# Mish layer on one core: the order of the first loads, with some of them behind TensorE's fillers

## The chip, the cores and the metric

The kernel runs on one core of a Trainium2 chip. A core has five engines, each with its own queue of instructions: TensorE (PE in the profile; PEld is its weight load), VectorE (DVE), ScalarE (ACT), GpSimd (POOL) and SyncE (SP). They meet only through semaphores. SP and ACT also issue DMAs; all of these run on the core's 16 DMA engines. The metric is the device time of one execution in microseconds, the median of several runs.

## The reference

```python
B, S, D, F = 1, 2048, 512, 1792          # all bfloat16
def reference(x, w1, b1, w2):
    h = jnp.einsum("bsd,df->bsf", x, w1) + b1
    sp = jnp.log1p(jnp.exp(-jnp.abs(h))) + jnp.where(h > 0, h, jnp.zeros_like(h))
    act = h * jnp.tanh(sp)
    return jnp.einsum("bsf,fd->bsd", act, w2)
```

A dense layer, the Mish activation, and a second dense layer. The first product contracts over D = 512, the second over F = 1792.

## The kernel before

**Tiles.** TensorE contracts over 128 partitions, so D is cut into KT = 4 slices (k 0 to k 3) and F into FT = 14 (f 0 to f 13). The 2048 rows of x are worked in four blocks of 512 (BLOCKS). For each block the first product makes, for every f, a tile of 128 values of F by 512 rows in one of the eight PSUM banks, with x transposed (xT) as the moving operand (mm1_step, L178). ScalarE adds b1 and applies Mish in one instruction and writes a_sb (mish, L161). The second product (mm2_step, L200) takes a_sb as weights, 128 rows at a time, and sums over the 14 f; VectorE copies the result out (put, L206), and a DMA stores it (L209).

**The order of work** is written out by hand: each engine has a Stream, which puts waits on semaphores into that engine's queue and gives each marked instruction a number. An engine works off its queue in order, so a wait holds all that stands behind it on the same engine.

**Loads.** All go through load (L85), which gives every DMA its own semaphore. SP's queue issues, in this order: x rows 0 to 255 as they are (x_nat), w1's k 1 for f 0 to 7, a DMA that transposes x rows 256 to 511 on the way into xT, w1's k 3 for f 0 to 7, b1, the rest of w1 (f 8 to 13, all k), w2, and three DMAs that transpose the other blocks of x. ACT's queue issues w1's k 0 and k 2 for f 0 to 7, once VectorE has zeroed b1_nat (t_bz, L102), and then loads the activation table (L125).

**The start on TensorE.** Eight matmuls on a constant (WARM: five of 512 columns, two of 256, one of 128; dummy, L131) fill the time until x is there. transpose_x (L147) then transposes x rows 0 to 255 with eight matmuls against an identity, and VectorE and ScalarE copy them from PSUM into xT (L152). The first block's first product starts on these rows, in an order that follows the loads (first): with k 0 four f on rows 0 to 127, the same four f on rows 128 to 255, then f 4 to 7 on both; with k 1 and then k 2 eight f on 256 rows each; then k 0, k 1 and k 2 on rows 256 to 511, eight f each; then k 3 on all 512 rows, whereupon Mish can run (spread_b1, L230 and L232, has spread b1 over the partitions by then). f 8 to 13 follow in the usual order (mm1), then the block's second product, and then the other three blocks.

Of the kernel before, what the change touches and what calls it, by code (L numbers as in the profile page):

```python
# [5 lines left out]
P = 128  # L6
SQ = 32
WARM = (512,) * 5 + (256,) * 2 + (128,)
# [24 lines left out]
def bass_standalone__dense_activation_mish__prompt_kernel(  # L33
# [8 lines left out]
    ACT = mybir.ActivationFunctionType  # L42
    ALU = mybir.AluOpType
    BF, F32 = dt.bfloat16, dt.float32
# [9 lines left out]
    OPEN = 8  # L54
    N0 = BLOCKS[0] // P

    with ExitStack() as es:
# [14 lines left out]
        ps = es.enter_context(nc.psum_tensor("ps", [P, 8, 512], F32))  # L72

        def sem(name):
            return es.enter_context(nc.semaphore(name))

        sp = Stream(nc.sync, None)
        pe = Stream(nc.tensor, sem("c_pe"))
        dve = Stream(nc.vector, sem("c_dve"))
        act = Stream(nc.scalar, sem("c_act"))  # L80
        pool = Stream(nc.gpsimd, sem("c_pool"))

        def load(q, dst, src, name, transpose=False):
            s = sem(name)
            (q.eng.dma_start_transpose if transpose else q.eng.dma_start)(dst, src).then_inc(s, 16)  # L85
            return (s, 16)

        def load_w1(q, ks, a, b):
            return load(q, w1_sb[:, ks, a * P:b * P], w1v[:, ks, a * P:b * P], "s_w1_%d_%d" % (ks.start, a))
# [6 lines left out]
        def load_part(q, k0, k1, a, b):  # L96
            t = load_w1(q, slice(k0, k1), a, b)
            for f in range(a, b):
                for k in range(k0, k1):
                    t_w1[k, f] = t  # L100

        t_bz = dve.mark(nc.vector.memset(b1_nat[:, :], 0.0))  # L102
        act.wait(t_bz)
        for k in (0, 2):
            load_part(act, k, k + 1, 0, OPEN)
        t_xn = load(sp, x_nat[:, :, :], x2[0:2 * P, :].rearrange("(p j) d -> p j d", p=P), "s_xn")
        load_part(sp, 1, 2, 0, OPEN)
        t_x23 = load(sp, xT[:, :, 2 * P:4 * P], x2[2 * P:4 * P, :], "s_x23", True)
        load_part(sp, 3, 4, 0, OPEN)
        sp.wait(t_bz)  # L110
# [11 lines left out]
        t_diff = pool.mark(pool.eng.iota(diff[:, :], pattern=[[1, P]], base=0, channel_multiplier=-1))  # L122
        dve.wait(t_diff)
        t_id = dve.mark(nc.vector.tensor_scalar(ident[:, :], diff[:, :], 0, None, ALU.is_equal))  # L124
        act.eng.preload_act_table(ACT.Mish)  # L125

        c_w = nc.const_aps.tensor(1.0, [P, P], BF)
        c_m = nc.const_aps.tensor(1.0, [P, 512], BF)

        def dummy(n):  # L130
            nc.tensor.matmul(ps[:, 7, 0:n], c_w, c_m[:, 0:n], start=True, stop=True)  # L131


        free = [[] for _ in range(8)]
        t_cp = {(j, k): t_x23 for j in (2, 3) for k in range(KT)}
# [2 lines left out]
        def transpose_x():  # L138

            pe.wait(t_xn, t_id)  # L140
            for bank, (eng, js, ks) in enumerate(((dve, (0,), (0,)), (act, (1,), (0,)), (dve, (0, 1), (1,)),
                                                  (act, (0, 1), (2, 3)))):
                n, m = len(ks), len(js)
                for i, k in enumerate(ks):
                    for h, j in enumerate(js):
                        lo = (i * m + h) * P
                        mm = nc.tensor.matmul(ps[:, bank, lo:lo + P], x_nat[:, j, k * P:(k + 1) * P], ident[:, :],  # L147
                                              start=True, stop=True)
                eng.wait(pe.mark(mm))
                dst = xT[:, ks[0]:ks[0] + n, js[0] * P:(js[-1] + 1) * P]  # L150
                src = ps[:, bank, 0:n * m * P].rearrange("p (k t) -> p k t", k=n)
                t = eng.mark(nc.vector.tensor_copy(dst, src) if eng is dve else act.eng.activation(dst, src, ACT.Copy))  # L152
                for k in ks:
                    for j in js:
                        t_cp[j, k] = t
                free[bank] = [t]
# [74 lines left out]
            dve.wait(t)  # L231
            return dve.mark(nc.vector.tensor_copy(b1_sb[:, :], b1_T[:, 0:FT]))  # L232

        for n in WARM:
            dummy(n)
        transpose_x()
        t_b1c = spread_b1()
        first(range(4), (0,), (0,))
# [48 lines left out]
```

## Time and profile before

| | |
|---|---|
| median of three runs | 104.51 us (104.5 to 105.24) |
| the profiled execution | 104.79 us |
| its span, first to last instruction | 103.4 us |
| TensorE busy | 100.3 us |
| ScalarE busy | 39.2 us |
| VectorE busy | 13.3 us |
| bytes by DMA | 7.94 MB |

The profile is of one execution. The span runs from the first to the last instruction; the rest of the time lies around it. Times in the views are microseconds from the span's start unless marked ns. A matmul's end in the profile is modelled, so the time from start to start says more of TensorE's pace than the length of one. An issue on SPq or ACTq lasts as long as the queue is taken up with it; the data arrive later, and the DMA view gives the time from issue to landing.

### The profile page before, as it was taken

The page shows a single profiled execution, that of the slowest core. Times are in us where ns is not written, and L with a number is a line of the kernel's source. Part 1 is how long each engine was busy: PE and PEld are TensorE (multiplying, and loading weights), DVE is VectorE, ACT ScalarE, POOL GpSimd, SP SyncE. Part 2 cuts the span into 40 slices and gives each one's busy share as a digit, 9 for nine tenths or more (in the row PEclk, how much of TensorE's full clock was granted, in tenths as well). Part 3 has the DMA queues.
Part 4 walks back from the last instruction along what each step waited for, and adds up shares of the span by engine and source line. Part 5 has one row for each costly group of instructions (what it writes and reads, how often), then busy time and mean ns, then how long its engine had stood idle before and what let it go on. Part 6 is the DMA issues. An engine that isn't in the chain of part 4 may idle for free.

```text
span 103.4 us, 1142 instructions
## 1 busy us (share of the span) xinstructions
PE 100.3 (97%) x497; PEld 49.1 (47%) x506; DVE 13.3 (13%) x26; ACT 39.2 (38%) x59; POOL 0.4 (0%) x5
## 2 busy tenths in 40 slices
PE   7999999999999999999999999999999999999992
PEld 2788444444444444444444444444444444444462
DVE  1203000211220000022220000022201000020223
ACT  2500999100037777100007777400005777700000
POOL 1000000000000000000000000000000000000000
PEclk9999999999999999999999999999999999999999
DMA  2999999991110000011011000001111000001111
GB/s 59 371 311 363 349 222 206 190 218 51 51 50 1 0 0 6 0 51 49 2 51 51 0 0 3 6 0 51 51 51 51 0 0 0 0 0 55 53 51 51
DMA packets 12833, 7.94 MB, mean 77 GB/s; under 512 B 7836, under 2 KB 12188, under 8 KB 12828
## 3 DMA queue, kind: packets, MB, share of 16 engines
q1 hardware_dynamic: 12396, 7.31, 27.4%
q10 hardware_dynamic: 432, 0.56, 1.6%
q8 instruction: 4, 0.07, 0.3%
q14 instruction: 1, 0.01, 0.0%
HBM read 3.94 MB, written 2.10 MB: 58 GB/s over the span
## 4 chain that ended last, share of the span: by engine, by line
PE 97%; issue 1%; DVE 0%
PE ps L178 47%; PE ps L200 47%; PE ps L131 3%; PE ps L147 1%; DVE o_sb L206 0%
## 5 line engine op out<-in xcount | busy, mean ns | idle before, releaser
L161 ACT ACTIVATE a_sb<-ps,b_sb 128x512 bf16<-128x512 f32 x56 | 37.1, 697 | 48.0 <-PE ps L178 42.8
L178 PE MATMUL ps<-xT,w_sb 128*128 128x512 bf16 (+2 forms) x247 | 49.0, 358 | 0.3
L200 PE MATMUL ps<-w_sb,a_sb 128*128 128x512 bf16 (+2 forms) x234 | 48.8, 367 | 0.2
L178 PEld LDWEIGHTS ps<-xT,w_sb 128*128 128x128 bf16 x252 | 24.5, 99 | 24.0
L200 PEld LDWEIGHTS ps<-w_sb,a_sb 128*128 128x128 bf16 x238 | 22.8, 98 | 26.0
L206 DVE CAST o_sb<-ps 128x512 bf16<-128x512 f32 (+2 forms) x17 | 11.2, 660 | 81.9 <-PE ps L200 81.9
L131 PE MATMUL ps<-const-bfloat16-1.0 128*128 128x512 bf16 (+2 forms) x8 | 2.8, 535 | 0.8 <-PEq L272 0.8
L131 PEld LDWEIGHTS ps<-const-bfloat16-1.0 128*128 128x128 bf16 x8 | 1.0, 140 | 2.2 <-issue 2.1
L125 ACT ACT_TABLE_LOAD x1 | 1.3, 1283 | 1.8 <-DVE ident L124 1.8
L152 ACT ACTIVATE xT<-ps 128x128 bf16<-128x128 f32 (+1 forms) x2 | 0.9, 437 | 1.1 <-PE ps L147 1.1
L230 DVE STREAM_TRANSPOSE b_T<-b_nat 32x32 bf16<-32x32 bf16 x4 | 0.8, 202 | 3.3 <-DMA b_nat<-in_b_dram 3.2
L147 PE MATMUL ps<-ident,x_nat 128*128 128x128 bf16 x8 | 1.0, 311 | 0.0
L152 DVE CAST xT<-ps 128x128 bf16<-128x128 f32 (+1 forms) x2 | 0.7, 358 | 2.5 <-PE ps L147 2.4
L147 PEld LDWEIGHTS ps<-ident,x_nat 128*128 128x128 bf16 x8 | 0.8, 142 | 0.2 <-DMA x_nat<-in_x_dram 0.2
L124 DVE TENSOR_SCALAR ident<-diff 128x128 bf16<-128x128 int32 x1 | 0.2, 226 | 0.2 <-POOL diff L122 0.2
L122 POOL IOTA diff<- 128x128 int32 x1 | 0.2, 234 | 0.4 <-POOLq L272 0.4
L102 DVE MEMSET b_nat<- 32x64 uint32 x1 | 0.1, 112 | 0.8 <-PEq L272 0.8
L232 DVE CAST b_sb<-b_T 128x14 f32<-128x14 bf16 x1 | 0.2, 175 | 0.0
L272 POOL MEMSET const-bfloat16-1.0<- 128x1 bf16 x1 | 0.1, 101 | 0.0
L272 POOL MEMSET const-uint8-127<- 128x1 uint8 x1 | 0.1, 101 | 0.0
L272 POOL MEMSET const-float32-0.0<- 128x1 f32 x1 | 0.1, 98 | 0.2 <-issue 0.2
L272 POOL MEMSET const-float32-1.0<- 128x1 f32 x1 | 0.1, 98 | 0.0
## 6 DMA issues: line engine op xcount, KB each, us to landing
out_dram<-o_sb SPq DMA_DIRECT2D x15, 128.0 KB, 1.7
w_sb<-in_w_dram SPq DMA_DIRECT2D x1, 1792.0 KB, 11.3
w_sb<-in_w_dram SPq DMA_DIRECT2D x1, 768.0 KB, 6.6
w_sb<-in_w_dram ACTq DMA_DIRECT2D x2, 256.0 KB, 3.8
w_sb<-in_w_dram SPq DMA_DIRECT2D x2, 256.0 KB, 4.0
x_nat<-in_x_dram SPq DMA_DIRECT2D x1, 256.0 KB, 2.6
out_dram<-o_sb SPq DMA_DIRECT2D x1, 96.0 KB, 1.6
xT<-in_x_dram SPq DMA_TRANSPOSE x4, 5.3
```

The costliest lines, as they stand in the source:

```text
L122: t_diff = pool.mark(pool.eng.iota(diff[:, :], pattern=[[1, P]], base=0, channel_multiplier=-1))
L124: t_id = dve.mark(nc.vector.tensor_scalar(ident[:, :], diff[:, :], 0, None, ALU.is_equal))
L125: act.eng.preload_act_table(ACT.Mish)
L131: nc.tensor.matmul(ps[:, 7, 0:n], c_w, c_m[:, 0:n], start=True, stop=True)
L147: mm = nc.tensor.matmul(ps[:, bank, lo:lo + P], x_nat[:, j, k * P:(k + 1) * P], ident[:, :], start=True, stop=True)
L152: t = eng.mark(nc.vector.tensor_copy(dst, src) if eng is dve else act.eng.activation(dst, src, ACT.Copy))
L161: t = act.mark(act.eng.activation(a_sb[:, f, starts[s]:starts[s + 1]], ps[:, bank, 0:n], ACT.Mish, bias=b1_sb[:, f:f + 1]))
L178: return nc.tensor.matmul(ps[:, bank, lo:hi], w1_sb[:, k, f * P:(f + 1) * P], xT[:, k, starts[s] + lo:starts[s] + hi], start=first, stop=( ...
L200: return nc.tensor.matmul(ps[:, bank, 0:hi - lo], a_sb[:, f, i * P:(i + 1) * P], w2_sb[:, f, lo:hi], start=(f == 0), stop=(f == FT - 1))
L206: t = dve.mark(nc.vector.tensor_copy(o_sb[:, i, lo:hi], ps[:, bank, 0:hi - lo]))
L230: t = dve.mark(nc.vector.transpose(b1_T[j * SQ:(j + 1) * SQ, :], b1_nat[:, j * SQ:(j + 1) * SQ]))
L272: nc = _bacc.Bacc("TRN2", target_bir_lowering=False, num_devices=1)
```

## The change

The table load becomes the first instruction on ACT. The eight fillers get a mark each, so that other engines can wait for them (t_fill). ACT still waits for the memset and issues k 0, but waits for the third filler before k 2. SP issues x_nat at once, waits for the second filler before k 1, and for the fifth before the DMA transpose; k 3, b1, the rest of w1, w2 and the other transposes stand behind that one as before. The fillers are put ahead in the program's text; on TensorE's queue they are first before and after. Nothing of the computation changes.

```diff
         t_bz = dve.mark(nc.vector.memset(b1_nat[:, :], 0.0))
+        c_w = nc.const_aps.tensor(1.0, [P, P], BF)
+        c_m = nc.const_aps.tensor(1.0, [P, 512], BF)
+
+        def dummy(n):
+            return nc.tensor.matmul(ps[:, 7, 0:n], c_w, c_m[:, 0:n], start=True, stop=True)
+
+        t_fill = [pe.mark(dummy(n)) for n in WARM]
+
+        act.eng.preload_act_table(ACT.Mish)
         act.wait(t_bz)
-        for k in (0, 2):
-            load_part(act, k, k + 1, 0, OPEN)
+        load_part(act, 0, 1, 0, OPEN)
+        act.wait(t_fill[2])
+        load_part(act, 2, 3, 0, OPEN)
         t_xn = load(sp, x_nat[:, :, :], x2[0:2 * P, :].rearrange("(p j) d -> p j d", p=P), "s_xn")
+        sp.wait(t_fill[1])
         load_part(sp, 1, 2, 0, OPEN)
+        sp.wait(t_fill[4])
         t_x23 = load(sp, xT[:, :, 2 * P:4 * P], x2[2 * P:4 * P, :], "s_x23", True)
         load_part(sp, 3, 4, 0, OPEN)
...
-        act.eng.preload_act_table(ACT.Mish)
-
-        c_w = nc.const_aps.tensor(1.0, [P, P], BF)
-        c_m = nc.const_aps.tensor(1.0, [P, 512], BF)
-
-        def dummy(n):
-            nc.tensor.matmul(ps[:, 7, 0:n], c_w, c_m[:, 0:n], start=True, stop=True)
...
-        for n in WARM:
-            dummy(n)
         transpose_x()
```

## The prediction, made before the result was known

> **What bounds the kernel now.** I read the page first, then the chain of waits in order of time, then the timeline of the first 16 us, then the DMA issues one by one.
>
> From the page: TensorE's share, its slices, and the DMA slices.
>
> ```profile
> PE 100.3 (97%) x497; PEld 49.1 (47%) x506; DVE 13.3 (13%) x26; ACT 39.2 (38%) x59; POOL 0.4 (0%) x5
> PE   7999999999999999999999999999999999999992
> DMA  2999999991110000011011000001111000001111
> ```
>
> From the chain of waits (start us, us, what):
>
> ```profile
> 0.73 0.04 issue
> 0.77 2.83 PE ps L131 x8
> 3.60 0.85 PE ps L147 x8
> 4.45 5.57 PE ps L178 x52
> 10.02 0.05 issue
> 10.07 6.86 PE ps L178 x31
> 16.93 3.88 PE ps L200 x18
> ...
> 101.59 0.02 issue
> 101.61 0.29 DVE o_sb L206
> ```
>
> The reader is to see that the chain never leaves TensorE: fillers (L131), transposes of x (L147), first product (L178), second product (L200), with nothing between them but gaps of 0.05 us, from 0.77 to 101.59 us. The 16 DMA engines are full until about 23 us (nine slices of 2.6 us). So the change can gain only if it makes TensorE start real work sooner, and it loses as soon as one load comes later than TensorE asks for it.
>
> This profiled execution took 104.79 us, 1.39 us of it outside the span of 103.4. The median of the runs is 104.51, so I add the change in the span to 104.51.
>
> **When each load is issued, when it lands, when it is asked for.** The timeline of the first 16 us (start us, us, engine, line, operation):
>
> ```profile
> 0.74 0.40 SPq L85 DMA_DIRECT2D x_nat<-in_x_dram  x1
> 0.95 0.87 ACTq L85 DMA_DIRECT2D w_sb<-in_w_dram  x2
> 1.20 0.41 SPq L85 DMA_DIRECT2D w_sb<-in_w_dram  x1
> 1.66 1.31 SPq L85 DMA_TRANSPOSE xT<-in_x_dram  x1
> 1.85 1.28 ACT L125 ACT_TABLE_LOAD   x1 [1.85 <-DVE ident L124]
> 3.02 0.57 SPq L85 DMA_DIRECT2D w_sb<-in_w_dram  x1
> 3.41 0.77 PEld L147 LDWEIGHTS ps<-ident,x_nat 128*128 128x128 bf16 x8 [0.19 <-DMA x_nat<-in_x_dram]
> 4.14 1.00 SPq L85 DMA_DIRECT2D w_sb<-in_w_dram  x2
> 4.26 12.02 PE L178 MATMUL ps<-xT,w_sb 128*128 128x128 bf16 x80
> 7.65 0.90 DVE L230 STREAM_TRANSPOSE b_T<-b_nat 32x32 bf16<-32x32 bf16 x4 [3.16 <-DMA b_nat<-in_b_dram]
> 8.59 0.17 DVE L232 CAST b_sb<-b_T 128x14 f32<-128x14 bf16 x1
> 10.34 5.88 ACT L161 ACTIVATE a_sb<-ps,b_sb 128x512 bf16<-128x512 f32 x10 [5.25 <-remote]
> ```
>
> The DMA view, asked around each issue in turn: x, w1's k 0, k 1, k 2, the DMA transpose of x rows 256 to 511, k 3, the rest of w1, w2. The last number is us from issue to landing.
>
> ```profile
> x_nat<-in_x_dram SPq DMA_DIRECT2D x1, 256.0 KB, 2.6
> w_sb<-in_w_dram ACTq DMA_DIRECT2D x1, 256.0 KB, 3.3
> w_sb<-in_w_dram SPq DMA_DIRECT2D x1, 256.0 KB, 3.7
> w_sb<-in_w_dram ACTq DMA_DIRECT2D x1, 256.0 KB, 4.4
> xT<-in_x_dram SPq DMA_TRANSPOSE x1, 5.0
> w_sb<-in_w_dram SPq DMA_DIRECT2D x1, 256.0 KB, 4.4
> w_sb<-in_w_dram SPq DMA_DIRECT2D x1, 768.0 KB, 6.6
> w_sb<-in_w_dram SPq DMA_DIRECT2D x1, 1792.0 KB, 11.3
> ```
>
> So x lands at 0.74 + 2.6 = 3.3, k 0 at 0.95 + 3.3 = 4.25, k 1 at 1.20 + 3.7 = 4.9, k 2 (the second of ACT's pair, about 1.4) at 5.8, the transposed rows at 1.66 + 5.0 = 6.7, k 3 at 7.4, the rest of w1 at 4.14 + 6.6 = 10.7, w2 (about 4.6) at 15.9.
>
> When TensorE asks for them follows from the shapes of the first products, here the matmuls grouped by form (busy us, mean ns), with the first row from 4.2 to 10 us:
>
> ```profile
> L178 PE MATMUL ps<-xT,w_sb 128*128 128x256 bf16 x44 | 5.0, 273 | 0.0
> L178 PE MATMUL ps<-xT,w_sb 128*128 128x128 bf16 x8 | 1.0, 297 | 0.0
> ```
>
> The 44 matmuls of 256 columns take 5.0 us, 0.113 each, and end where the chain has its gap at 10.02; so they began at 5.06. Four of them belong to k 0, then come 8 of k 1, 8 of k 2 and 24 on the transposed rows. k 1 is asked for at 5.06 + 4 x 0.113 = 5.5, k 2 at 6.4, the transposed rows at 7.3, k 3 at 10.07. In the chain from 10.07 eight matmuls of k 3 come ahead of the rest of w1; 31 take 6.86, so 8 take 1.77, and the rest of w1 is asked for at 11.8, w2 at 16.9. Slack today: k 1 0.6, k 2 0.6, transposed rows 0.6, rest of w1 1.1, w2 1.0. x and k 0 have none: k 0 lands as the first product starts.
>
> **The change part by part.**
>
> *The fillers and their marks.* The same eight matmuls stand first on TensorE before and after, and no queue is ahead of them; five semaphore marks more cost nothing that I can find a row for. Their price lies between 0 and the 0.05 of one of the chain's gaps; I take 0. Moving text that stands on other engines changes nothing on TensorE's queue.
>
> *x and k 0 alone at first.* x will land somewhat sooner than 3.3. What that can buy is the 0.19 us that the weight load waited for x at 3.41. But the matmuls were not idle then: the chain has the fillers and the transposes without a gap, and fillers stand ahead in the same queue. The gain lies between 0 and 0.19; I take 0. k 0 too may land sooner, and buys nothing: the transposes' eight matmuls end only as the first product starts.
>
> *The table load ahead of k 0 on ACT.* The load has 1.28 us and will start about 0.75, where the queues of SP and TensorE start. The trace of before has it behind the two DMA issues, never ahead, so it doesn't show whether a DMA issue waits for it. One end: it doesn't, and k 0 is issued at 0.95 as today, behind the same memset. Other end: it does, and k 0 is issued at 0.75 + 1.28 = 2.03. Then it lands 2.6 (x's row) to 3.3 (its own row) later, at 4.6 to 5.3, and the first product stalls 0.4 to 1.1. I take the first end, because the profile books the table load to the engine (ACT) and DMA issues to its queue (ACTq), two rows that need not wait for each other.
> [...]
>
> *k 1 behind the second filler, k 2 behind the third, the transpose behind the fifth.* Their ends, from the timeline asked at 1.25, 0 to 2, and 2.7 us:
>
> ```profile
> 0.77 1.01 PE L131 MATMUL ps<-const-bfloat16-1.0 128*128 128x512 bf16 x2 [0.77 <-PEq L272]
> 0.77 1.44 PE L131 MATMUL ps<-const-bfloat16-1.0 128*128 128x512 bf16 x3 [0.77 <-PEq L272]
> 2.43 0.64 PE L131 MATMUL ps<-const-bfloat16-1.0 128*128 128x512 bf16 x1
> ```
>
> Second at 1.78, third at 2.21, fifth at 3.07. So k 1 goes from 1.20 to 1.8, k 2 from 1.4 to 2.2, the transpose from 1.66 to 3.1. Behind the transpose on SP's queue stand k 3, b1, the rest of w1, w2 and three further transposes: all 1.41 later. Behind k 2's wait on ACT stand only the two copies of the transposed x at 3.85 and 4.49, over a us away.
>
> The late end: each load takes as long from issue to landing as today. k 1 lands at 5.5, asked for at 5.5: 0. k 2 at 6.6 against 6.4: 0.2. The transposed rows at 3.07 + 5.0 = 8.1 against 7.3: 0.8. k 3 at 8.8 against 10.07: 0. b1's spreading, which ended at 8.76, ends at 10.17, before the first activation at 10.34: 0. The rest of w1 at 12.1 against 11.8 and w2 at 17.3 against 16.9 are late by less than the 0.8 that the rows have by then put TensorE back. So the late end is 0.8 in all, not a sum.
>
> The early end counts bytes. Today those long times are mostly queueing, as the stretches of the start show (us, then busy times, last the DMA share and GB/s):
>
> ```profile
> 1.65:2.65 1.00, 1.00 (x4) 0.39 (x3) 0.00 (x0) 0.80 (x1) 0.00 (x0) 1.00 0.79 176
> 2.65:4.95 2.30, 2.30 (x19) 1.77 (x18) 0.72 (x2) 1.22 (x3) 0.00 (x0) 1.00 1.05 382
> 4.95:6.70 1.75, 1.75 (x20) 1.58 (x18) 0.00 (x0) 0.14 (x1) 0.00 (x0) 1.00 1.16 278
> ```
>
> 176 + 2.3 x 382 = 1055 KB by 4.95 is x, k 0, k 1 and k 2 (four times 262 KB). The transposed rows are today the fifth 262 KB, and stay so. If the engines never run dry, they end at 4.95 + 262/278 = 5.9, plus the time from the last byte to the semaphore, and land by about 6.7 as today. Do they run dry? A load's bytes start 0.9 us behind its issue (x: 0.74, first bytes at 1.65). x and k 0, 524 KB, last until 2.65 + 348/382 = 3.6; k 1 has bytes from 2.7, k 2 from 3.1, the transpose from 4.0, k 3 (issued 4.4) from 5.3, the rest of w1 (5.55) from 6.4. Each is there before the one ahead of it is through. So the early end is 0, and I take it: the rows of DMA share (1.05, 1.16) are nearer to a full queue than to a fixed latency. If that cover goes, the transposed rows are what is late first, at 7.3.
>
> **Sum.** 0 + 0 + 0 + 0: span 103.4, time 104.5. Between the ends of all parts: -0.19 to +1.1.
>
> **Rivals.**
> *Transposed rows late (slower).* Place: the 24 matmuls at 7.3. It decides once the rows land more than 0.6 later than now, that is if more than 0.6 of the 1.41 us of later issue comes through to the landing. For it: the issue alone takes 1.31 us, and nothing can be hidden twice. Against: the byte count. At its price, up to 0.8, the time is 105.3.
> *k 0 waits for the table load (slower).* Place: the first product at 4.26. It decides as soon as k 0 is issued more than a few hundredths later, as there is no slack. Price 0.4 to 1.1, middle 0.7: 105.2.
> [...]
> *A late clock.* From 4.26 on eight matmuls of 128 columns take from 4.26 to 5.06, 0.1 each, and then ones of 256 columns 0.113: TensorE doubles its pace at about 5.0, 4.2 us after its first filler. If a stall before 5.0 puts that step off by as much again, 4.2 us at half pace cost 2.1: with the 0.7 of the stall 107.3. [...]
> *A gain from earlier x.* The 0.19 comes through: 104.3. Against it the gapless chain at 3.4.
>
> **How the numbers follow.** No change 0.72 (its own range 104.2 to 104.9); transposed rows late 0.11; k 0 behind the table 0.10; ACT held twice as long 0.01; clock 0.02; gain 0.04. The range 104.2 to 105.4 takes in the likeliest, the gain, the late rows and over half of k 0's case. A measurement of this kernel can tell about 1%, 1.05 us. Faster by more than that (under 103.46): no case reaches it, 0.01. Slower (over 105.55): the clock, the long hold of ACT, the upper part of k 0's case, and a late load together with k 0, 0.10. Within: 0.89.
>
> **What the profile after would show.** Right: k 0 issued on ACTq at 0.95 beside the table load; no idle time on TensorE before 5.5 us; the transposed rows landing before 7.3, about 3.6 after their issue; the chain on TensorE alone. Wrong: ACTq's first issue at 2.0 and L178 waiting for w_sb at 4.3; or L178 waiting for xT at 7.3; or 256 columns taking over 0.2 us after 5.1; or, for a gain, L147 starting before 3.4.

## The result and the profile after

The changed kernel takes 105.82 us (median of 14 runs, 105.24 to 106.43); the kernel before, run beside it, 104.89 (14 runs, 104.35 to 105.64). The ratio is 1.0083, with a 95% interval of 1.0058 to 1.0108: slower by 0.9 us, less than 1% but clear of noise. The forecast was no change, 104.5 in 104.2 to 105.4, and the time lies outside that range. The profiled execution took 106.0 us with a span of 104.7.

The chain of waits of the changed kernel:

```profile
0.73 0.04 issue
0.77 1.03 PE ps L107 x2
1.80 0.02 issue
1.82 4.86 DMA w_sb<-in_w_dram
6.67 0.05 issue
6.72 4.54 PE ps L182 x40
11.26 0.05 issue
11.31 6.85 PE ps L182 x31
18.17 3.88 PE ps L204 x18
```

Where the chain was TensorE alone, it now goes from the second filler (L107) into a load of w1 that takes 4.86 us, and from that into the first product (L182). The timeline names the load and shows what became of each issue:

```profile
0.73 1.28 ACT L111 ACT_TABLE_LOAD   x1 [0.73 <-PEq L274]
0.95 1.63 ACTq L85 DMA_DIRECT2D w_sb<-in_w_dram  x2
1.82 0.33 SPq L85 DMA_DIRECT2D w_sb<-in_w_dram  x1
3.10 1.31 SPq L85 DMA_TRANSPOSE xT<-in_x_dram  x1
3.42 0.71 PEld L151 LDWEIGHTS ps<-ident,x_nat 128*128 128x128 bf16 x8 [0.20 <-DMA x_nat<-in_x_dram]
4.20 1.08 PE L182 MATMUL ps<-xT,w_sb 128*128 128x128 bf16 x12
6.72 9.50 PE L182 MATMUL ps<-xT,w_sb 128*128 128x256 bf16 x62 [1.44 <-DMA w_sb<-in_w_dram]
```

k 0 is issued at 0.95 beside the table load, as forecast. The twelve matmuls of k 0 run from 4.20 to 5.28. Then TensorE stands still for 1.44 us and begins k 1 at 6.72. The load is k 1, issued at 1.82. The DMA view, asked around each issue (x, k 0, k 1, k 2, the DMA transpose; last the us from issue to landing):

```profile
x_nat<-in_x_dram SPq DMA_DIRECT2D x1, 256.0 KB, 2.6
w_sb<-in_w_dram ACTq DMA_DIRECT2D x1, 256.0 KB, 3.1
w_sb<-in_w_dram SPq DMA_DIRECT2D x1, 256.0 KB, 4.9
w_sb<-in_w_dram ACTq DMA_DIRECT2D x1, 256.0 KB, 4.7
xT<-in_x_dram SPq DMA_TRANSPOSE x1, 4.7
```

k 1 needed 3.7 us when it was issued at 1.20, and needs 4.9 when it is issued later, with no more queued ahead of it. x, now with k 0 alone beside it, still needs 2.6. The stretches of the start, first of the changed kernel and then of the kernel before (last the DMA share and GB/s, both counted by the packets that start in the stretch):

```profile
1.65:2.65 1.00, 1.00 (x4) 0.39 (x3) 0.00 (x0) 0.36 (x1) 0.00 (x0) 1.00 0.44 170
2.65:3.65 1.00, 1.00 (x7) 0.53 (x6) 0.00 (x0) 0.00 (x0) 0.00 (x0) 1.00 1.00 373
3.65:4.65 1.00, 1.00 (x17) 0.97 (x16) 0.72 (x2) 0.58 (x2) 0.00 (x0) 1.00 0.87 145
4.65:5.65 1.00, 0.63 (x7) 0.28 (x4) 0.00 (x0) 0.29 (x1) 0.00 (x0) 1.00 1.14 366
5.65:6.65 1.00, 0.00 (x0) 0.00 (x0) 0.00 (x0) 0.00 (x0) 0.00 (x0) 1.00 1.11 162
```

```profile
2.65:3.65 1.00, 1.00 (x7) 0.54 (x6) 0.00 (x0) 0.48 (x1) 0.00 (x0) 1.00 1.04 379
3.65:4.65 1.00, 1.00 (x12) 0.93 (x11) 0.72 (x2) 0.44 (x2) 0.00 (x0) 1.00 1.06 401
4.65:5.65 1.00, 1.00 (x13) 0.94 (x11) 0.00 (x0) 0.44 (x1) 0.00 (x0) 1.00 1.16 267
5.65:6.65 1.00, 1.00 (x12) 0.90 (x10) 0.00 (x0) 0.00 (x0) 0.00 (x0) 1.00 1.18 314
```

Until 3.65, x and k 0, the two kernels move the same. Then, where k 1 should follow, the engines move 145 GB/s in place of 401, although k 1 had been issued 1.8 us earlier; 256 KB are missing by 4.65, the size of one load. A DMA share of 0.87 with 145 GB/s says that the engines are busy with packets that last long, not that they have none. The trace's packet records, read one by one, bear this out. In both kernels the first packets of k 1 start at 3.5 us. Of the 71 packets of 2 KB that start from 3.65 to 4.65 in the changed kernel, 52 take the usual 0.08 to 0.09 us, but 15 take 0.3 us or more, up to 1.07; in the kernel before 196 start there, and the longest takes 0.27. A second poor stretch follows at 5.65.

### The profile page after: what moved, and what is told of

The parts are those of the page before. It is cut to its first block, busy times and chain, and to the rows that moved or that the text cites. A ratio compares the mean times of both kernels' runs of the same rounds, so it can differ in the third digit from the quotient of the medians.

```text
span 104.7 us, 1142 instructions
## 1 busy us (share of the span) xinstructions
PE 100.1 (96%) x497; PEld 48.7 (47%) x506; DVE 13.3 (13%) x26; ACT 39.3 (37%) x59; POOL 0.4 (0%) x5
## 4 chain that ended last, share of the span: by engine, by line
PE 92%; DMA 5%; issue 1%; DVE 0%
PE ps L204 46%; PE ps L182 45%; DMA w_sb<-in_w_dram 5%; PE ps L107 1%; DVE o_sb L210 0%
## 5 line engine op out<-in xcount | busy, mean ns | idle before, releaser
L182 PE MATMUL ps<-xT,w_sb 128*128 128x512 bf16 (+2 forms) x247 | 48.9, 355 | 1.7 <-DMA w_sb<-in_w_dram 1.4
L182 PEld LDWEIGHTS ps<-xT,w_sb 128*128 128x128 bf16 x252 | 24.2, 98 | 25.6 <-DMA w_sb<-in_w_dram 1.6
L107 PE MATMUL ps<-const-bfloat16-1.0 128*128 128x512 bf16 (+2 forms) x8 | 2.8, 535 | 0.8 <-PEq L274 0.8
L107 PEld LDWEIGHTS ps<-const-bfloat16-1.0 128*128 128x128 bf16 x8 | 1.0, 140 | 2.2 <-issue 2.1
L151 PE MATMUL ps<-ident,x_nat 128*128 128x128 bf16 x8 | 0.9, 279 | 0.0
L151 PEld LDWEIGHTS ps<-ident,x_nat 128*128 128x128 bf16 x8 | 0.7, 133 | 0.2 <-DMA x_nat<-in_x_dram 0.2
```

The costliest lines, as they stand in the source:

```text
L107: return nc.tensor.matmul(ps[:, 7, 0:n], c_w, c_m[:, 0:n], start=True, stop=True)
L182: return nc.tensor.matmul(ps[:, bank, lo:hi], w1_sb[:, k, f * P:(f + 1) * P], xT[:, k, starts[s] + lo:starts[s] + hi], start=first, stop=( ...
```

## The experiments

Each is the changed kernel with the edit shown, unless it says otherwise. The table sums them up: when k 1, k 2 and the transpose of rows 256 to 511 are issued, GB/s from 3.65 to 4.65 us, when k 1 and k 2 land (issue plus the DMA view's time), and the ratio to the kernel before on the same chip. Landings and GB/s are of one profiled execution each. The ratios of e2, e4, g2 and h1 rest on four executions, that of f4 on two, the others on six to fourteen.

| kernel | k 1 | k 2 | rows | GB/s | k 1, k 2 land | ratio (95% interval) |
|---|---|---|---|---|---|---|
| before | 1.2 | 1.4 | 1.7 | 401 | 4.9, 5.8 | 1 |
| changed | 1.8 | 2.2 | 3.1 | 145 | 6.7, 6.9 | 1.0083 (1.0058 to 1.0108) |
| e1 table only | 1.2 | 1.4 | 1.7 | 401 | 4.9, 5.7 | 1.0006 (0.9967 to 1.0045) |
| e2 k 1, k 2 wait | 1.8 | 2.2 | 2.2 | 268 | 5.2, 6.9 | 1.0121 (1.0059 to 1.0182) |
| e3 rows wait | 1.2 | 1.4 | 3.1 | 404 | 4.8, 5.5 | 1.0021 (0.9984 to 1.0058) |
| e4 plain rows | 1.8 | 2.2 | 3.1 | 186 | 6.4, 6.6 | 1.0107 (1.0053 to 1.0161) |
| e5 k 1, rows wait | 1.8 | 1.4 | 3.1 | 352 | 6.0, 5.8 | 1.0029 (0.9998 to 1.006) |
| e6 k 2, rows wait | 1.2 | 2.2 | 3.1 | 348 | 4.7, 5.6 | 1.0049 (1.0016 to 1.0081) |
| e7 both on SP | 1.8 | 2.2 | 3.1 | 178 | 6.0, 6.8 | 1.0051 (1.0022 to 1.0081) |
| e8 waits a filler sooner | 1.4 | 1.8 | 3.1 | 395 | 4.8, 5.6 | 1.0032 (1.0005 to 1.0059) |
| f1 swapped | 1.8 | 2.2 | 3.1 | 74 | 6.7, 6.9 | 1.0082 (1.0061 to 1.0103) |
| f2 waits a filler later | 2.2 | 2.7 | 3.1 | 154 | 6.4, 6.7 | 1.0081 (1.0051 to 1.0112) |
| f3 k 3 first | 1.8 | 2.2 | 3.1 | 279 | 6.7, 7.0 | 1.0111 (1.0078 to 1.0143) |
| f4 e2, plain | 1.8 | 2.2 | 2.2 | 133 | 6.7, 6.9 | 1.0127 (1.0058 to 1.0195) |
| g1 k 2 behind the fifth | 1.8 | 3.1 | 3.1 | 234 | 4.8, 6.6 | 1.0074 (1.0028 to 1.012) |
| g2 one load | 1.8 | 1.8 | 3.1 | 217 | 6.7 | 1.0108 (1.0039 to 1.0176) |
| g3 behind the first | 1.4 | 1.4 | 3.1 | 375 | 5.5, 5.7 | 1.0006 (0.9966 to 1.0046) |
| h1 spaced | 1.8 | 2.7 | 3.6 | 217 | 6.7, 7.4 | 1.0127 (1.0063 to 1.019) |

**Which wait costs the time (e1 to e4).** Two theories stood against each other. A: while SP issues the transpose, the engines hardly move data, and the fifth filler's wait has put that stretch upon k 1. B: k 1 and k 2 themselves are issued too late.

e1 is the kernel before with the table load alone moved:

```diff
+        act.eng.preload_act_table(ACT.Mish)
         act.wait(t_bz)
...
-        act.eng.preload_act_table(ACT.Mish)
```

> The kernel before with the table load alone put first on ACT; no wait on a filler. All theories: ACTq issues k 0 at 0.95 us as before, every load lands as before (k 1 by 4.9, transposed rows by 6.7), TensorE without idle time, ratio to the kernel before 1.000 within its interval. If the table load has a part in the loss, k 1 or k 0 lands later and the ratio is 1.003 or more.

As expected: k 0 is issued at 0.95, k 1 lands at 4.9, and the table load's place costs nothing that these runs can tell (the interval reaches from 0.9967 to 1.0045).

e2 takes the transpose's wait away, e3 leaves it as the only one:

```diff
-        sp.wait(t_fill[4])            # e2
-        sp.wait(t_fill[1])            # e3
-        act.wait(t_fill[2])           # e3
```

> The changed kernel without the wait for the fifth filler: k 1 and k 2 still wait for the second and third filler, the transpose follows k 1 on SP at about 2.15 us. Theory A (while SP issues a transpose, the 16 engines hardly move data, wherever that falls): the poor stretch moves from 3.7-4.6 to about 2.4-3.4 us, onto x and k 0; k 1 lands by 5.5, the first product may start some tenths late; ratio 1.000 to 1.006. Theory B (k 1 and k 2, issued late, leave the engines dry): k 1 lands at about 6.5 as in the changed kernel and TensorE waits over 1 us for it; ratio 1.008 or more.

> The changed kernel with the wait for the fifth filler alone: k 1 and k 2 are issued at about 1.2 and 1.4 us as before, the transpose at 3.1. Theory A: GB/s fall below 200 between 3.6 and 4.6 us as in the changed kernel, k 1 lands at 5.6 or later (asked for at 5.5), transposed rows at 7.6; ratio 1.003 to 1.009. Theory B: no poor stretch, k 1 by 4.9, transposed rows by 6.8; ratio 1.000.

e3 moves as much as the kernel before, here its stretches and its chain, with TensorE alone in it:

```profile
3.65:4.65 1.00, 1.00 (x12) 1.00 (x10) 0.72 (x2) 0.44 (x2) 0.00 (x0) 1.00 1.05 404
```

```profile
0.77 2.82 PE ps L107 x8
3.60 0.85 PE ps L149 x8
4.45 5.40 PE ps L180 x52
9.85 0.05 issue
9.90 6.96 PE ps L180 x31
```

e2 is as slow as the changed kernel, e3 is not. The transpose's wait alone shows no cost, and the loss is that of k 1's and k 2's. In e2's profile k 1 landed in time and k 2 was the late one, which B had not said. But the profiled execution is the fastest of e2's four (105.42 us; the others took 106.35 to 106.41), so it may not be typical of them.

e4 puts a plain DMA of the same bytes in the transpose's place:

```diff
-        t_x23 = load(sp, xT[:, :, 2 * P:4 * P], x2[2 * P:4 * P, :], "s_x23", True)
+        t_x23 = load(sp, xT[:, :, 2 * P:4 * P],
+                     x2[2 * P:4 * P, :].rearrange("(p a) (b c) -> p (a b) c", p=P, c=2 * P), "s_x23")
```

> The changed kernel with a plain DMA of the same 256 KB in place of the first DMA transpose, at the same place and behind the same wait (rows 256 to 511 are then not transposed, so their part of the output is another one). Theory A: no poor stretch at 3.7-4.6, k 1 lands by 5.0, k 2 by 5.9, no idle time on TensorE; ratio 1.000. Theory B: k 1 still lands after 6 us; ratio 1.008.

As slow without a transpose there: theory A falls, B holds.

**Both or one (e5 to e8).** C: the two hold each other up. D: any load issued after the first bytes move comes slowly. (The prediction and the expectations put the first bytes at 1.65, which is where their stretch begins; in the traces the first packet starts at about 1.77.)

```diff
-        act.wait(t_fill[2])           # e5
-        sp.wait(t_fill[1])            # e6
...
         load_part(sp, 1, 2, 0, OPEN)
+        load_part(sp, 2, 3, 0, OPEN)  # e7, and ACT's wait and load of k 2 go
...
-        sp.wait(t_fill[1])            # e8
+        sp.wait(t_fill[0])
-        act.wait(t_fill[2])
+        act.wait(t_fill[1])
```

> The changed kernel without ACT's wait for the third filler: k 2 is issued at about 1.4 us, k 1 still at 1.8, the transpose at 3.1. Theory C (k 1 and k 2, issued close together on two queues, hold each other up): k 2 now goes ahead, lands by 5.1, and k 1 by 5.8; TensorE waits 0.3 us at most; ratio under 1.004. Theory D (a load issued after the engines have begun to move x, about 1.7 us, comes slowly, whatever the other does): k 1 lands after 6.0, TensorE waits 0.5 us or more; ratio 1.006 or more.

> The changed kernel without SP's wait for the second filler: k 1 is issued at 1.2 us, k 2 at 2.2, the transpose at 3.1. Theory C: k 1 by 4.9, k 2 by 5.9, no idle time on TensorE; ratio 1.000 to 1.002. Theory D: k 1 by 4.9, but k 2 at 6.5 or later, asked for at 6.4; TensorE waits 0.1 to 0.6 us; ratio 1.002 to 1.006.

> The changed kernel with k 2 on SP's queue right behind k 1 (issued at about 1.8 and 2.2 us, so both late, but on one queue and one after the other), and only k 0 on ACT. Theory C: k 1 by 5.0, k 2 by 5.9, no idle time on TensorE; ratio 1.000. Theory D: k 1 after 6.0, over 0.5 us of waiting; ratio 1.006 or more.

> The changed kernel with each of the two waits one filler sooner: k 1 behind the first (about 1.4 us), k 2 behind the second (about 1.8), the transpose at 3.1 as before. Theory C: still close together on two queues, so k 1 after 5.8; ratio 1.004 or more. Theory D: k 1 is issued ahead of the first bytes and lands by 5.0; k 2 is late, 6.3 or more, 0 to 0.4 us of waiting; ratio 1.000 to 1.005.

Neither theory stands. With one of the two loads late (e5, e6, e8) the engines keep 348 to 395 GB/s, against D, and a late k 2 lands by 5.6. e5 still has 0.80 us of waiting for k 1, which now stands behind k 2 and lands at 6.0 (its interval just takes in no change). With both late they don't, even on one queue in sequence (e7), against C as it was put. What TensorE waits for in e6's profile is another load, as its timeline says: the rest of w1, 1.4 us later behind the transpose, lands at 12.2, and TensorE waits for it.

```profile
12.33 1.02 PE L181 MATMUL ps<-xT,w_sb 128*128 128x512 bf16 x4 [0.26 <-DMA w_sb<-in_w_dram]
```

**Why both (f1 to f4).** J: bytes flow fully only 2 to 2.5 us after an issue. F: a load is slow if its own queue has begun to be worked off. K, for the second poor stretch: the transpose stands still while some engines are at a plain load.

```diff
-        act.wait(t_fill[2])           # f1: k 1 on ACT, k 2 on SP
-        load_part(act, 2, 3, 0, OPEN)
+        act.wait(t_fill[1])
+        load_part(act, 1, 2, 0, OPEN)
-        sp.wait(t_fill[1])
-        load_part(sp, 1, 2, 0, OPEN)
+        sp.wait(t_fill[2])
+        load_part(sp, 2, 3, 0, OPEN)
...
-        sp.wait(t_fill[1])            # f2
+        sp.wait(t_fill[2])
-        act.wait(t_fill[2])
+        act.wait(t_fill[3])
...
+        load_part(sp, 3, 4, 0, OPEN)  # f3: k 3 here, not behind the transpose
         sp.wait(t_fill[1])
```

f4 has the edits of e2 and e4 together.

> The changed kernel with the queues of the two late loads swapped: k 1 on ACT behind k 0, after the second filler (about 1.8 us); k 2 on SP behind x, after the third (2.2). Theory J (bytes flow at full rate only some 2 to 2.5 us after an issue, on either queue; x and k 0 are through at 3.5, so a k 1 issued at 1.8 leaves the engines dry until about 4.3): under 250 GB/s from 3.65 to 4.65, k 1 lands after 5.5, TensorE waits 0.3 us or more for it; ratio 1.004 or more. Theory F (a load is slow if its own queue has begun to be worked off when it is issued, as SP's has at 1.7 and ACT's not before 2.8): k 1 on ACT by 5.0, k 2 on SP after 6.3; over 300 GB/s from 3.65 to 4.65; ratio under 1.004.

> The changed kernel with both waits one filler later: k 1 behind the third (2.2 us), k 2 behind the fourth (2.65), the transpose at 3.1 as before. Theory J: the dry stretch grows by about 0.4 us, k 1 lands 0.2 to 0.6 later than in the changed kernel or its e4 form (6.4 to 6.7), TensorE starts k 1 at 6.6 to 7.2; ratio 1.010 to 1.018. Theory F: as the changed kernel but for the later issue of k 1; the same sign, so this run sizes the loss and doesn't tell J from F.

> The changed kernel with k 3 put at SP's front, right behind x (issued at 1.2 us); k 1 and k 2 still wait for the second and third filler, the transpose for the fifth. Theory J: k 3's bytes keep the engines fed from 3.5 to 4.2, over 340 GB/s from 3.65 to 4.65; k 1, a load later in line, lands at 5.4 to 6.0, so TensorE still waits up to 0.5 us, and k 3 has lost its lateness; ratio 1.002 to 1.006. Theory F: under 250 GB/s from 3.65 to 4.65 or from 4.2 to 5.2, k 1 after 6.2; ratio 1.008 or more.

> The kernel of e2 (k 1 and k 2 wait, rows 256 to 511 don't) with a plain DMA in place of the first DMA transpose, so that part of the output is another one. In e2 the engines fell to 81 GB/s from 5.65 to 6.65 us and k 2 landed at 6.9. Theory K (the transpose's bytes stand still while some engines are still at a plain load, and hold that load's completion up): over 250 GB/s from 5.65 to 6.65, k 2 by 6.3. If K is wrong and k 2 is late by its issue alone, it lands at 6.6 to 6.9 again.

F falls: on ACT's queue k 1 is as late, and the stretch is the poorest of all.

```profile
3.65:4.65 1.00, 1.00 (x12) 1.00 (x11) 0.72 (x2) 0.36 (x2) 0.00 (x0) 1.00 0.68 74
6.74 0.94 PE L182 MATMUL ps<-xT,w_sb 128*128 128x256 bf16 x7 [0.51 <-DMA w_sb<-in_w_dram]
```

Whichever queue issues them, the two come late: k 1 lands at 6.7 in f1 and at 6.0 in e7, k 2 at 6.9 and 6.8. J misses too: one filler more cost nothing more (f2, 1.0081), and in f3, where k 3 was to feed the engines meanwhile, k 1 landed at 6.7 and the ratio was 1.0111. K is half right: with a plain load the second stretch has 353 GB/s where e2 has 81, yet k 1 and k 2 land at 6.7 and 6.9 all the same.

```profile
5.65:6.65 1.00, 0.87 (x8) 0.53 (x6) 0.00 (x0) 0.00 (x0) 0.00 (x0) 1.00 1.15 81
5.65:6.65 1.00, 0.59 (x3) 0.11 (x1) 0.00 (x0) 0.00 (x0) 0.00 (x0) 1.00 1.08 353
```

So the second stretch is not needed for the loss. In the changed kernel it has a hand in it all the same. The trace has k 1's landing in sixteen parts: four arrive by 5.64 and twelve from 6.49 to 6.68, just as fifteen of the transpose's 256-byte packets, after up to 0.95 us each, end together at 6.50 to 6.53.

**What bound there is (g1 to g3, h1).** L: when x and k 0 are through at 3.5, the next load must be one that was issued before the first bytes. M: two issues close together spoil each other. N, formed after g1 and g2: 512 KB issued within half a us are too much, 256 KB at a time are not.

```diff
-        act.wait(t_fill[2])           # g1
+        act.wait(t_fill[4])
...
-        act.wait(t_fill[2])           # g2
-        load_part(act, 2, 3, 0, OPEN)
-        load_part(sp, 1, 2, 0, OPEN)
+        load_part(sp, 1, 3, 0, OPEN)
...
-        sp.wait(t_fill[1])            # g3
+        sp.wait(t_fill[0])
-        act.wait(t_fill[2])
+        act.wait(t_fill[0])
...
-        act.wait(t_fill[2])           # h1
+        act.wait(t_fill[3])
-        sp.wait(t_fill[4])
+        sp.wait(t_fill[7])
```

> The changed kernel with k 2 behind the fifth filler instead of the third (issued at about 3.1 us), k 1 still behind the second (1.8). Theory L (when x and k 0 are through at 3.5 us, the next load in line must be one that was issued before the first bytes at 1.65; a later one starts poorly): under 250 GB/s from 3.65 to 4.65, k 1 after 5.5. Theory M (two issues close together, while the engines already move data, spoil both): k 1 is alone, over 300 GB/s while it moves, and it lands by 5.0; k 2 at 6 to 7. Either way k 2 is late, asked for at 6.4; ratio 1.002 to 1.012.

> The changed kernel with k 1 and k 2 in one DMA of 512 KB on SP behind the second filler (1.8 us), only k 0 on ACT. Theory L: still under 250 GB/s from 3.65 to 4.65, since the one load is late and nothing else is there; it lands at 6.3 or later; ratio 1.006 or more. Theory M: one issue, so over 330 GB/s from 3.65 to 4.65 and landing at 5.5 to 6.0, when TensorE asks for k 1 at 5.5; ratio 1.000 to 1.004.

> The changed kernel with both waits on the first filler: k 1 and k 2 are issued at about 1.4 us, both ahead of the first bytes at 1.65; the transpose stays behind the fifth. Theory L: over 380 GB/s from 3.65 to 4.65, k 1 by 4.9, k 2 by 5.8, no idle time on TensorE; ratio 1.000. Theory M and the first theories of a loss by mere closeness: k 1 after 5.5; ratio 1.005 or more.

> The changed kernel with the three waits spread out: k 1 behind the second filler (1.8 us), k 2 behind the fourth (2.65), the transpose behind the eighth (about 3.6). No two of them within 0.8 us. Theory N (after the engines have begun, 512 KB issued within about half a us come poorly, 256 KB at a time don't; in g1 k 1 alone moved well, and k 2 and the transpose, issued together at 3.1, did not; in g2 one load of 512 KB did not either): over 330 GB/s from 3.65 to 4.65, k 1 by 5.0, k 2 by 6.0; what is left is the transposed rows at 7.3 or somewhat later; ratio 1.000 to 1.004. Theory L (lateness as such): k 1 moves well as in g1, but k 2 behind it poorly, under 250 GB/s from 4.3 to 5.3 and k 2 after 6.4; ratio 1.004 or more.

g3 shows what undoes the loss: with both loads issued at 1.4 us there is none that its runs can tell (1.0006, up to 1.0046), and its chain is TensorE alone. k 1's last part landed at 5.5 there, and in this execution TensorE came to k 1 at 5.96.

```profile
3.65:4.65 1.00, 1.00 (x12) 1.00 (x11) 0.72 (x2) 0.43 (x2) 0.00 (x0) 1.00 1.03 375
4.46 13.29 PE ps L182 x84
```

M falls with g2, one issue and as slow; N, as it was put, with h1, well spaced and as slow. L does not fit all rows: in e2 and g1 k 1, late and next in line, landed at 5.2 and 4.8, while h1, with the same issue of k 1, has it at 6.7:

```profile
3.65:4.65 1.00, 1.00 (x12) 1.00 (x11) 0.72 (x2) 0.44 (x2) 0.00 (x0) 1.00 0.87 217
6.73 0.94 PE L182 MATMUL ps<-xT,w_sb 128*128 128x256 bf16 x7 [1.06 <-DMA w_sb<-in_w_dram]
```

And f3, where the early k 3 was next in line, was slow none the less. So shown is this: in all eleven kernels in which both k 1 and k 2 are issued at 1.8 us or later, one of them lands at 6.6 to 7.4 and TensorE waits for one of them; in the seven with at least one of them issued at 1.4 or earlier, both land by 6.0 and the ratio is 1.005 at most. The slow eleven have 1.005 to 1.013, so the two groups touch in time (e6 and e7) but not in landings. The packet records part them as well: the longest of the 2 KB packets that start from 3.65 to 4.65 takes 0.86 to 1.24 us in the eleven and at most 0.45 in the seven.

Why packets last so long in the second group of loads, and when a single late load escapes it, stays open. Whether the first bytes are what marks the time is not shown either, since neither of the two was issued between 1.4 and 1.8. One form of N was not tested by itself: that two late loads spoil each other when they are in the engines together, however far apart they were issued. In h1 the late packets on ACT's queue start at 3.99, while k 1's start from 3.39 to 5.67; in g1 they start at 4.32, when k 1's last starts at 4.42.

## Why the prediction was wrong, point by point

- **The step that failed** is "Do they run dry? ... Each is there before the one ahead of it is through. So the early end is 0, and I take it". It gave every late load the 0.9 us that it read for x from issue to first bytes (1.0 in the trace, 0.74 to 1.77), and from then on the rate of a full queue, 382 GB/s. The first half held: k 1's packets start at 3.5, as k 0's end. The rate did not: measured from 3.65 to 4.65 are 145 GB/s, and k 1 lands at 6.7, 1.2 after TensorE asks for it by the prediction's 5.5. That is the loss against the profile before: 6.72 - 5.5 = 1.2, against 104.7 - 103.4 = 1.3 in the span. Why the rate fell stays open, as said above.
- **The late end was no bound.** "Each load takes as long from issue to landing as today" gave k 1 5.5 and a price of 0. With 4.9 us in place of 3.7 it is past both ends, and so the time was past the range. The bound held only if a load issued later, with no more ahead of it, takes no longer; the rows show that it can.
- **No rival was it.** "Transposed rows late" has the right kind of cause, a late issue that comes through, but the wrong load: they landed at 3.10 + 4.7 = 7.8, while TensorE, held by k 1, came to them only some 1.8 us after 6.72; with their wait alone (e3) there is no loss. "k 0 waits for the table load" didn't happen: ACTq's issue stands at 0.95 beside the table load, which lasts from 0.73 to 2.01 (e1 as well). That ACT is held for twice the load's time, the 0.01 in the sum of chances, no run shows: in the changed kernel ACT's queue issues k 0 at 0.95 and k 2 at 2.25, while twice 1.28 us from 0.73 would end at 3.3. That the table load's engine and the queue's issues need not wait for each other was right.
- **The clock.** In the changed kernel's profile TensorE doubled its pace at about 4.0, ahead of the stop, and kept it: after the stop 40 matmuls take 4.54 us, the same 0.113 each as before. f1 comes nearer to the rival: its matmuls of 256 columns still start 0.213 us apart when the stop comes at about 6 us, and 0.110 apart behind it. So that stop put the step off by no 4.2 us. A stall before 5.0, which the rival asked for, no run has; that a stall puts the step off at all was the author's assumption and is not shown. The sign "256 columns taking over 0.2 us after 5.1" is no sign of a stall: e1 and g3 have such matmuls until 6.2 and 6.6 without any.
- **x and k 0 alone** bought nothing, as forecast, and for a reason more: x takes 2.6 us with or without k 1, k 2 and the transpose behind it, and L151 starts at 3.42 as L147 did at 3.41.
- **The rest of w1** was given 12.1 against 11.8 as its late end. e6 shows that end: 12.2, and 0.26 of waiting. In the changed kernel k 1's wait covers it.
- **The signs.** k 0 at 0.95 beside the table load came out right. No idle time before 5.5, rows before 7.3 and a chain on TensorE alone did not, and of the signs of being wrong none named w_sb at the start of k 1, where the wait is.
- **The size.** The medians differ by 0.9 and the profiled spans by 1.3. The runs of before spread over 1.3 us (104.35 to 105.64), and the 1.3 is the difference of two single executions. Of the 1.3 between forecast and measurement 0.4 is the base: 104.51 was the median of three executions, 104.89 is that of fourteen. The 0.6 of slack, too, belongs to one execution: TensorE comes to k 1 at 5.5 in the profile before, at 5.1 in the changed kernel's and at 5.96 in g3's, by when its pace steps up (last section). Once k 1 is what TensorE waits for, that no longer counts: the changed kernel and f1 idle 1.44 and 0.51 us, begin k 1 at 6.72 and 6.74, and have the same median, 105.82.

## What to carry to other kernels

Queue up front, here by 1.4 us, the loads that the first microseconds of work need; holding some back doesn't make the first ones land sooner (x: 2.6 us either way) and made the held ones take up to 1.2 us longer. When a load is moved later, its time from issue to landing may grow although no more stands ahead of it (k 1: from 3.7 to 4.9 us), so its time in the old place is no upper bound; ask what slack the asking engine has (here about 0.6 us) and hold the load back by clearly less: k 1 held back by 0.2 cost nothing that shows (g3), by 0.6 it was waited for (e5). And where a chain of waits is one engine without a gap, a change in the loads can hardly win and has each load's slack to lose.

## What the runs showed of the hardware that was not expected

The engines can be busy and move little: a DMA share of 0.87 with 145 GB/s in the changed kernel, 0.68 with 74 in f1, against 1.06 with 401 in the kernel before. In the changed kernel's stretch it is single packets of 2 KB that take up to 1.07 us in place of 0.08.

TensorE's pace steps up at a time that differs from one profiled execution to the next. e1 has the order of work of the kernel before; its chain has the 52 matmuls of 128 and 256 columns at

```profile
4.45 6.20 PE ps L178 x52
```

where the kernel before has 5.57 and e3 has 5.40, with no idle time in any of them. From one start to the next, matmuls of 128 columns go from 0.107 to 0.056 us and those of 256 from 0.213 to 0.110. They do so at about 4.65 us in e3, 5.0 in the kernel before and 6.3 in e1; among all the profiles the step lies between 3.5 (f3) and 6.7 (g3). The PEclk column of the stretches reads 1.00 on both sides of it, so only the spacing shows it. While TensorE waits for no load, each us of a later step costs half a us: the 1.3 us between the steps of e1 and the kernel before are 0.63 in the 52 matmuls, the whole difference of their profiled times, 105.42 and 104.79. A step anywhere in those 3.2 us would account for the 1.3 us over which the kernel before spreads; that each of its executions differs by this was not seen, as one was profiled. What sets the time of the step these runs don't show.
